# Attention and two feed-forward layers on one core: reloads behind their stores, two early tiles moved, the last tile transposed on TensorE

## The chip, the core and the metric

The kernel runs on one core of one Trainium2 chip. The metric is the device time of one execution in microseconds; smaller is better. A core has TensorE (PE; its weight loads are PEld), VectorE (DVE), ScalarE (ACT), GpSimd (POOL), SyncE (SP, which here only issues DMAs), SBUF as working memory, and PSUM, into which TensorE writes.

## What is computed

The input is attention data `q`, `k`, `v` of 4 x 8 x 576 x 64. The output of the attention is reshaped to 2304 rows (tokens) of 512 numbers, which go through two layers:

```python
x = ...                         # attention: a coarse part (4 positions averaged) + a local part (a band of 7)
h = x @ w_in                    # 512 -> 2048
g = h * tanh(softplus(h))
x = g @ w_out                   # 2048 -> 512
h = x @ moe2_w_in               # 512 -> 1024
solu = h * softmax(h)           # over the 1024 columns of a row
ln = (solu - mean) / sqrt(var + 1e-06) * g_ln
out = ln @ moe2_w_out           # 1024 -> 512
```

Attention and the first layer are not touched by the change; the second layer is.

## The kernel before

**Numbers.** Every matrix product is done with both operands split into a high and a low part of 32-bit "fp32r" numbers, and three products are added (`PASS`: high x high, high x low, low x high). So one tile of the second layer's input product is 2 x 12 matmuls of 512 columns, and one of its output product 24.

**First layer.** The 2304 tokens go in five blocks of 512, 384, 384, 512 and 512. A block has 16 chunks of the hidden dimension. A chunk is 12 matmuls into PSUM `h` (`chunk_in`, L631), an element-wise chain of five ACT and three DVE steps (L639 to L648), which ends with the cast L647 and the difference L648 that make the high and low half of `g`, and 12 matmuls into PSUM `y` (`chunk_out`, L659). At the end of a block `y` is copied out of PSUM with its sign turned, one half by ACT (L676), one by DVE (L673), and stored to the DRAM scratch `yscr` (`block_end`).

**Second layer.** Its weights are decoded beside the first layer, stored to scratch, loaded again and split (`second_split`, which calls `split`: cast L553 on ACT, difference L554 on DVE). Then 18 tiles of 128 tokens follow, each in two parts:

- `tile_in` (L682): load the tile from `yscr` into `qu` or `ku` by turns; split it (cast L691, difference L692 into `raw`); 24 matmuls (L700) into PSUM `y` (tiles 0 and 1: into two PSUM tiles `at`); row maximum L724 on DVE (L714 in tiles 0 and 1), exponential L726 (L719) on ACT, two products L729 on DVE, square with sum L737 on ACT, some small steps (L732 to L752), and the normalised tile, half by DVE (L759), half by ACT (L761). It has tokens on the partitions, and the output product needs the hidden dimension there. So it is stored to the scratch `zscr` (one DMA of 512 KB), loaded again in four DMAs of 128 KB that exchange 32 x 32 blocks, and transposed within the blocks by DVE (L771, two halves), each half followed by the cast L774 on ACT and the difference L775 on DVE, which make the two parts of `ln`.
- `tile_out` (L779): 24 matmuls (L787) of `ln` with the second weights, a copy L792 out of PSUM by ACT, and the store of the result.

All DMAs of this part are issued by SP through one helper (L266 in the profile).

**What sets the order.** No engine's order is written out by hand. Each step is recorded by `Plan.op` with an engine, a cost in us, a wanted time and the buffers that it reads and writes. `Plan.run` then plays the program through with these costs: whenever an engine is free, it takes, among the steps whose inputs are ready and for which buffers are free, the one wanted earliest. The order that results is the order in which the instructions are issued, engine by engine; on the chip each engine takes them strictly in this order. For a DMA `run` takes as its end the data time plus 1.3 us early in the program and 4.0 us later (`end = dma + (1.3 if now < 150 else 4.0)`). Wanted times are counted in chunks ("slots") of the first layer, 80 in all: tile `t` is wanted at `80 + 3 * (t - 2)`, but tiles 0 and 1 at 80 + `INTO[t]`, so among the last chunks, and the output part `G2LAG` = 10 later than the input part:

```python
INTO = (-5.5, -2.5)
s = 16 * NB + (INTO[t] if t < 2 else 3 * (t - 2))
pe(24 * 0.216, s + G2LAG, g2, [ln] + [w4t[k][0] for k in range(8)], [o])
```

## Time and profile before

| | |
|---|---|
| device time, median of 3 runs | 753.57 us (750.67 to 753.71) |
| the profiled execution | 748.23 us, of which 746.4 us are the profile's span |
| TensorE busy | 700.1 us (94%), mean granted clock 0.972 |
| DVE, ACT, POOL busy | 477.4, 484.2, 71.9 us |
| DMA | 99.40 MB, mean 133 GB/s |

The page gives the busy time of each engine; the chain in order of time shows, step by step backwards from the end, what released what; the waits list who waited for whom; the timeline shows instructions with the idle time before them and its releaser in brackets; the windows give the busy time and the granted TensorE clock (1.00 is full speed) of chosen stretches. A group "x24" is 24 instructions in a row. The second layer's tiles begin near 500 us, between the last chunks of the first layer.

### The profile page before, as it was taken

To read this page: it belongs to the slowest core of one execution; us is meant where nothing else is said; L and a number is where in the kernel's file an instruction comes from. 1 tells how busy PE (TensorE), PEld (TensorE's weight loads), DVE (VectorE), ACT (ScalarE), POOL (GpSimd) and SP (SyncE) were. 2 spreads that over 40 slices of the span, in tenths; PEclk is the share of its full clock that TensorE was granted. 3 is DMA by queue.
4 is the path that set the end of the run, shared out by engine and by line. 5 is a ranking of instruction groups with operands and counts; after the bars stand their busy time and mean duration, and the time that the engine had idled before them with its cause. 6 is when DMAs were issued, how large, how long until landed. Compare 5 with 4: busy or idle time off the path is not lost.

```text
span 746.4 us, 14379 instructions
## 1 busy us (share of the span) xinstructions
PE 700.1 (94%) x5576; PEld 585.4 (78%) x5576; DVE 477.4 (64%) x1040; ACT 484.2 (65%) x1143; POOL 71.9 (10%) x86
## 2 busy tenths in 40 slices
PE   3668999899999999999999999999999899999997
PEld 2456777799898899898788888888778688888875
DVE  6787897778745357665666665436645666666662
ACT  2785887677776687777686677667634554555542
POOL 2033333122310011200000000000000000000000
PEclk9757999999999999999999999999999999999999
DMA  8998764745623057643233314112234354345332
GB/s 243 264 289 210 184 140 106 261 99 134 123 49 111 18 125 190 161 142 130 79 105 122 103 43 161 67 69 68 88 114 142 111 156 143 130 138 169 128 113 99
DMA packets 76252, 99.40 MB, mean 133 GB/s; under 512 B 6616, under 2 KB 58712, under 8 KB 76184
## 3 DMA queue, kind: packets, MB, share of 16 engines
q1 hardware_dynamic: 64152, 84.66, 36.2%
q0 software_dynamic: 9440, 9.10, 8.5%
q10 hardware_dynamic: 2592, 4.72, 1.6%
q8 instruction: 44, 0.72, 0.4%
q14 instruction: 24, 0.20, 0.1%
HBM read 74.34 MB, written 24.12 MB: 132 GB/s over the span
## 4 chain that ended last, share of the span: by engine, by line
PE 80%; DMA 6%; ACT 5%; DVE 5%; issue 2%; SPq 1%; POOL 0%; ACTq 0%; POOLq 0%
PE h L631 24%; PE y L659 23%; PE at L787 13%; PE y L700 12%; DMA qkd<-in_qkc_dram 2%; PE at L410 2%; DMA wi<-in_w_dram 2%; DMA wo<-in_vc_dram 2%; PE at L700 1%; SPq L266 1%; PE at L484 1%; ACT sm L374 1%; PE at L353 1%; PE at L526 1%; PE at L513 1%
## 5 line engine op out<-in xcount | busy, mean ns | idle before, releaser
L631 PE MATMUL h<-x,wi 128*128 128x512 f32 (+1 forms) x960 | 215.7, 374 | 5.8 <-DVE e L645 5.7
L659 PE MATMUL y<-g,wo 128*128 128x512 f32 (+1 forms) x960 | 218.4, 374 | 1.8 <-ACT g L647 1.2
L631 PEld LDWEIGHTS h<-x,wi 128*128 128x128 f32 x960 | 174.5, 189 | 32.5 <-DVE e L645 8.1
L659 PEld LDWEIGHTS y<-g,wo 128*128 128x128 f32 x960 | 173.3, 189 | 27.6 <-ACT g L647 2.0
L787 PE MATMUL at<-wi,wo 128*128 128x512 f32 x432 | 103.4, 395 | 6.1 <-ACT wo L774 6.0
L787 PEld LDWEIGHTS at<-wi,wo 128*128 128x128 f32 x432 | 81.7, 190 | 25.7 <-ACT wo L774 7.2
L700 PE MATMUL y<-wi,raw 128*128 128x512 f32 x384 | 89.4, 389 | 0.8 <-ACT vu L676 0.8
L700 PEld LDWEIGHTS y<-wi,raw 128*128 128x128 f32 x384 | 72.0, 188 | 16.1 <-ACT vu L676 1.2
L639 ACT ACTIVATE e<-h 128x512 f32<-128x512 f32 (+1 forms) x80 | 44.1, 551 | 54.5 <-PE h L631 54.0
L645 DVE SCALAR_TENSOR_TENSOR e<-e,h 128x512 f32<-128x512 f32 (+1 forms) x80 | 50.4, 631 | 33.6 <-ACT e L644 33.0
L641 ACT ACTIVATE e<-e,ones 128x512 f32<-128x512 f32 (+1 forms) x80 | 54.3, 680 | 17.8 <-DVE e L640 17.5
L648 DVE TENSOR_TENSOR g<-e,g 128x512 fp32r<-128x512 f32 (+1 forms) x80 | 50.7, 635 | 22.6 <-ACT g L647 22.0
L647 ACT CAST g<-e 128x512 fp32r<-128x512 f32 (+1 forms) x80 | 45.9, 575 | 27.9 <-DVE e L645 27.7
L640 DVE TENSOR_SCALAR e<-e 128x512 f32<-128x512 f32 (+1 forms) x80 | 31.8, 397 | 43.3 <-ACT e L639 43.1
L643 ACT ACTIVATE e<-e,ones 128x512 f32<-128x512 f32 (+1 forms) x80 | 54.2, 679 | 1.6
L264 POOL DMA_DIRECT2D qkd<-in_qkc_dram x36 | 35.5, 996 | 133.7 <-DMA qkd<-in_qkc_dram 79.7
L644 ACT ACTIVATE e<-e 128x512 f32<-128x512 f32 (+1 forms) x80 | 46.9, 586 | 1.1
L726 ACT ACTIVATE wo<-y,nm 128x1024 f32<-128x1024 f32 x16 | 17.9, 1116 | 37.4 <-DVE nm L724 37.4
L264 POOL DMA_DIRECT2D vd<-in_vc_dram x36 | 36.3, 1020 | 58.5 <-DMA vd<-in_vc_dram 37.7
L374 ACT ACTIVATE sm<-sm,nm 128x40 f32<-128x40 f32 x120 | 37.6, 315 | 4.8 <-DVE nm L368 4.8
L737 ACT ACTIVATE wo<-wo,mv 128x1024 f32<-128x1024 f32 x18 | 20.7, 1152 | 22.7 <-DVE mv L732 22.7
L729 DVE SCALAR_TENSOR_TENSOR wo<-wo,y 128x512 f32<-128x512 f32 x32 | 21.7, 683 | 17.8 <-ACT wo L726 17.8
(151 smaller groups left out, 806.3 us busy)
## 6 DMA issues: line engine op xcount, KB each, us to landing
raw<-in_w_dram SPq DMA_DIRECT2D x24, 512.0 KB
zscr<-wo SPq DMA_DIRECT2D x18, 512.0 KB
wo<-zscr SPq DMA_DIRECT2D x72, 128.0 KB
wi<-in_w_dram SPq DMA_DIRECT2D x6, 1024.0 KB
wo<-in_w_dram SPq DMA_DIRECT2D x6, 1024.0 KB
qkd<-in_qkc_dram POOLq DMA_DIRECT2D x36, 144.0 KB, 4.7
ku<-in_ku_dram SPq DMA_DIRECT2D x15, 320.0 KB
vu<-in_vu_dram SPq DMA_DIRECT2D x60, 80.0 KB
```

Source lines behind the costliest of these rows:

```text
L264: return op("pool", nbytes / DMA_RATE, want, lambda: nc.gpsimd.dma_start(out_(), in_(), accum_op=ALU.add), r, w, after=after)
L374: nc.scalar.activation(heads()[:, i, :], heads()[:, i, :], AF.Exp, bias=nm()[:, i:i + 1], accum_out=su()[:, i:i + 1])
L631: mm(h()[:, :N], w()[:, f % 2, a, 128 * c:128 * c + 128], x()[:, b, c, :N], start=(n == 0), stop=(n == 11))
L641: act(act_us(N, 0.09), s + 0.1, lambda: nc.scalar.activation(e(), e(), AF.Square, bias=ones()[:, 0:1]), [ones], [eb])
L643: lambda: nc.scalar.activation(e(), e(), AF.Ln, scale=0.5, bias=ones()[:, 1:2]), [ones], [eb])
L644: act(act_us(N), s + 0.1, lambda: nc.scalar.activation(e(), e(), AF.Exp, scale=-1.0), [], [eb])
L645: dve(dve_us(N), s + 0.2, lambda: nc.vector.scalar_tensor_tensor(e(), e(), 1.0, h()[:, :N], op0=ALU.subtract, op1=ALU.mult), [h], [eb])
L647: act(act_us(N), s + 0.2, lambda: nc.scalar.copy(g()[:, 0, :N], e()), [eb], [g])
L648: dve(dve_us(N), s + 0.2, lambda: nc.vector.tensor_tensor(g()[:, 1, :N], e(), g()[:, 0, :N].bitcast(F32), op=ALU.subtract), [eb], [g])
L659: mm(y[d2]()[:, d, :N], w()[:, f % 2, a, c:c + 128], g()[:, b, :N], start=(f == fs[0] and n == 0), stop=(f == fs[-1] and n == 2))
L700: mm(part(m), x()[:, a, c, :], w()[:, i, b, :], start=(n == 0), stop=(n == 11))
L787: mm(o(), ln()[:, a, k, :], w()[:, i, b, :], start=(n == 0), stop=(n == 23))
```

## The change

Four things are changed in the plan's inputs, and one in what is computed where.

- `op` and `dma` take a `lag` for SP's DMAs, the time that the plan adds behind the data. The store to `zscr` gets 0.3 and the four reloads 1.0 in place of 4.0, so that in the plan a reload becomes ready soon after its store.
- `INTO` becomes (-7, -0.9): tile 0 is wanted earlier, tile 1 later.
- The output part of tiles 0 and 1 is wanted 8 instead of 10 slots behind their input part.
- The last tile (t = 17) is not stored and loaded again. It is normalised into its plain order, transposed by eight TensorE transposes of 128 x 128 into two PSUM tiles `h`, and cast (L780 of the changed kernel) and differenced (L781) from there.

```diff
--- before.py
+++ after.py
@@ -42,7 +42,7 @@
 NEXT = {0: (0.0, 6.0, -3.0, 0.8), 26: (-3.0, 4.0, -14.0, 2.0), 32: (2.0, 10.0, 4.0, 1.2), 48: (2.0, 10.0, 4.0, 1.2)}
 WANT = [0, 2, 4, 6, 8, 13, 16, 20]
 G2LAG = 10
-INTO = (-5.5, -2.5)
+INTO = (-7, -0.9)
 DMA_RATE = 270e3
 LAG = 0.15
 AHEAD = 2
@@ -99,7 +99,6 @@
         self.ops = []
 
     def op(self, eng, cost, want, fn, r=(), w=(), lag=None, after=(), join=False):
-        lag = LAG if lag is None else lag
         n = len(self.ops)
         deps = set(after)
         for b in r:
@@ -169,10 +168,10 @@
                     if eng in ("sp", "pool"):
                         at[eng] = now + (0.45 if eng == "sp" else 1.1)
                         dma = max(dma, at[eng] + 1.2) + cost
-                        end = dma + (1.3 if now < 150 else 4.0)
+                        end = dma + ((1.3 if now < 150 else 4.0) if lag is None else lag)
                     else:
                         at[eng] = now + cost
-                        end = at[eng] + lag
+                        end = at[eng] + (LAG if lag is None else lag)
                         heapq.heappush(done, (at[eng], pick, True))
                     heapq.heappush(done, (end, pick, False))
             nxt = [t for e, t in at.items() if t > now and ready[e]]
@@ -257,13 +256,13 @@
     yparts = [[Buf(None, None, None, 0) for _ in range(2)] for _ in range(NB)]
     wparts = [Buf(None, None, None, 0) for _ in range(8)]
 
-    def dma(want, out_, in_, r=(), w=(), nbytes=0, accum=False, after=(), pool=False, join=False):
+    def dma(want, out_, in_, r=(), w=(), nbytes=0, accum=False, after=(), pool=False, join=False, lag=None):
         if pool:
             return op("pool", nbytes / DMA_RATE, want, lambda: nc.gpsimd.dma_start(out_(), in_()), r, w, after=after, join=join)
         elif accum:
             return op("pool", nbytes / DMA_RATE, want, lambda: nc.gpsimd.dma_start(out_(), in_(), accum_op=ALU.add), r, w, after=after)
         else:
-            return op("sp", nbytes / DMA_RATE, want, lambda: nc.sync.dma_start(out_(), in_()), r, w, after=after, join=join)
+            return op("sp", nbytes / DMA_RATE, want, lambda: nc.sync.dma_start(out_(), in_()), r, w, lag, after, join)
 
     def dve(cost, want, fn, r, w, after=()):
         return op("dve", cost, want, fn, r, w, after=after)
@@ -754,17 +753,39 @@
         act(0.35, s + 0.3, root, [], [r])
         dve(0.6, s + 0.4, stat, [mv], [r])
         ln = S([128, 2, 8, 128], "wo", 8, F32R)
-        turned = lambda m: ez()[:, 1].rearrange("t (g k f) -> t g k f", g=4, k=8)[:, :, 4 * m:4 * m + 4]
-        flat = lambda m: e()[:, m].rearrange("t (k g f) -> t g k f", k=4, g=4)
+        last = t == NTI - 1
+        flat = lambda m: e()[:, m] if last else e()[:, m].rearrange("t (k g f) -> t g k f", k=4, g=4)
+
+        def turned(m):
+            if last:
+                return ez()[:, 1, 512 * m:512 * m + 512]
+            return ez()[:, 1].rearrange("t (g k f) -> t g k f", g=4, k=8)[:, :, 4 * m:4 * m + 4]
+
         dve(dve_us(512), s + 0.4, lambda: nc.vector.tensor_scalar(
             turned(0), flat(0), mv()[:, 2:3], y(), op0=ALU.add, op1=ALU.mult), [mv, r], [ez])
         act(act_us(512), s + 0.4, lambda: nc.scalar.activation(
             turned(1), flat(1), AF.Identity, bias=c(), scale=y()), [r], [ez])
-        dma(s + 0.5, lambda: zscr[t], lambda: ez()[:, 1], r=[ez], w=[zs], nbytes=524288)
+        if last:
+            for m in range(2):
+                tp = P("h")
+                ks = slice(4 * m, 4 * m + 4)
+
+                def flip(m=m, tp=tp):
+                    for k in range(4):
+                        nc.tensor.transpose(tp()[:, 128 * k:128 * k + 128],
+                                            turned(m)[:, 128 * k:128 * k + 128], ident())
+
+                pe(0.43, s + 0.9, flip, [ez, ident], [tp])
+                v = lambda tp=tp: tp().rearrange("f (k t) -> f k t", k=4)
+                act(act_us(512), s + 0.9, lambda v=v, ks=ks: nc.scalar.copy(ln()[:, 0, ks, :], v()), [tp], [ln])
+                dve(dve_us(512), s + 0.9, lambda v=v, ks=ks: nc.vector.tensor_tensor(
+                    ln()[:, 1, ks, :], v(), ln()[:, 0, ks, :].bitcast(F32), op=ALU.subtract), [tp], [ln])
+            return ln
+        dma(s + 0.5, lambda: zscr[t], lambda: ez()[:, 1], r=[ez], w=[zs], nbytes=524288, lag=0.3)
         for g in range(4):
             dma(s + 0.6, lambda g=g: zv()[32 * g:32 * g + 32],
                 lambda g=g: zscr[t].rearrange("(a t) (g f) -> g t a f", a=4, g=4)[g],
-                r=[zs, ez], w=[zv], nbytes=131072, join=True)
+                r=[zs, ez], w=[zv], nbytes=131072, join=True, lag=1.0)
         for m in range(2):
             ks = slice(4 * m, 4 * m + 4)
             v = lambda ks=ks: ez()[:, 1].rearrange("p (k t) -> p k t", k=8)[:, ks]
@@ -787,7 +808,7 @@
                     mm(o(), ln()[:, a, k, :], w()[:, i, b, :], start=(n == 0), stop=(n == 23))
                     n += 1
 
-        pe(24 * 0.216, s + G2LAG, g2, [ln] + [w4t[k][0] for k in range(8)], [o])
+        pe(24 * 0.216, s + (8 if t < 2 else G2LAG), g2, [ln] + [w4t[k][0] for k in range(8)], [o])
         os_ = S([128, 512], "ys", 2)
         act(act_us(512), s + 1.6, lambda: nc.scalar.copy(os_(), o()), [o], [os_])
         op("act", 0.1, s + 1.6, lambda: nc.scalar.dma_start(out[128 * t:128 * t + 128, :], os_()), [os_], (), lag=5.0)
```

The instructions themselves are otherwise the same; what else changes is their order, which the plan makes. The order up to TensorE's row 254 is the same in both. Lines of the changed kernel up to L755 are one less than before (L699 is L700 before), the two halves of the normalised tile are L764 and L766 (L759 and L761 before), the transposes, casts and differences L792, L795 and L796 (L771, L774, L775), the output product L808 (L787).

TensorE at the end of the last block, before (`h` and `y` are the first layer's chunks, `y<-wi,raw` and `at<-wi,raw` a second-layer tile's input product, `at<-wi,wo` its output product; x24 is one tile):

```order
L659 MATMUL y<-g,wo 128x512 x12
L631 MATMUL h<-x_4658,wi 128x512 x12
L659 MATMUL y<-g,wo 128x512 x24
L700 MATMUL y<-wi,raw 128x512 x48
L787 MATMUL at<-wi,wo 128x512 x48
```

and with the change:

```order
L658 MATMUL y<-g,wo 128x512 x12
L630 MATMUL h<-x_4658,wi 128x512 x12
L699 MATMUL at<-wi,raw 128x512 x24
L658 MATMUL y<-g,wo 128x512 x24
L699 MATMUL y<-wi,raw 128x512 x24
L808 MATMUL at<-wi,wo 128x512 x24
L699 MATMUL y<-wi,raw 128x512 x48
```

Tile 1's input product now stands between the last `h` and the last 24 `y` matmuls, and behind these one input and one output product follow in place of two and two.

SP in the first tiles, before (`zscr<-wo` is a tile's store, `wo<-zscr` with the same number its four reloads, `ku`, `qu<-yscr` the load of a later tile; wo_6139 and wo_6194 are tiles 2 and 3):

```order
L266 DMA ku_6188<-yscr_66 128x4x128
L266 DMA zscr_68<-wo_6139 128x1024
L266 DMA zscr_68<-wo_6194 128x1024
L266 DMA wo_6139<-zscr_68 32x4x256 x4
L266 DMA qu_6310<-yscr_66 128x4x128
L266 DMA wo_6194<-zscr_68 32x4x256 x4
```

and with the change (wo_6044, wo_6147 and wo_6225 are tiles 1, 2 and 3):

```order
L265 DMA wo_6044<-zscr_68 32x4x256 x4
L265 DMA zscr_68<-wo_6147 128x1024
L265 DMA ku_6220<-yscr_66 128x4x128
L265 DMA wo_6147<-zscr_68 32x4x256 x4
L265 DMA qu_6277<-yscr_66 128x4x128
L265 DMA zscr_68<-wo_6225 128x1024
```

Each tile's reloads now follow its own store, ahead of the next tile's store. DVE in the same place, before (L724 is the row maximum of tile 5, L771 the transposes of tile 2, L729 the products of tile 5):

```order
L724 TENSOR_REDUCE nm2_6338<-y_6294 128x1
L740 SCALAR_TENSOR_TENSOR r2_6342<-mv_6327,su2_6313 128x1
L771 STREAM_TRANSPOSE wo_6139<-wo_6139 128x4x4x32
L729 SCALAR_TENSOR_TENSOR wo_6344,mv_6350<-wo_6344,y_6294 128x512
L775 TENSOR_TENSOR wo_6348<-wo_6139,wo_6348 128x512
L749 TENSOR_SCALAR r2_6342<-r2_6342 128x1
L750 TENSOR_SCALAR r2_6342<-r2_6342 128x1
L751 TENSOR_TENSOR r2_6342<-r2_6342 128x1
L752 TENSOR_TENSOR r2_6342<-r2_6342,mv_6327 128x1
```

and with the change, from right behind the row maximum of tile 4 (L792 are the transposes of tile 2, L728 the products of tile 4, L748 to L764 the normalisation of tile 3, L691 the low half of tile 5's input):

```order
L792 STREAM_TRANSPOSE wo_6147<-wo_6147 128x4x4x32
L728 SCALAR_TENSOR_TENSOR wo_6284,mv_6292<-wo_6284,y_6207 128x512
L748 TENSOR_SCALAR r2_6282<-r2_6282 128x1
L749 TENSOR_SCALAR r2_6282<-r2_6282 128x1
L750 TENSOR_TENSOR r2_6282<-r2_6282 128x1
L751 TENSOR_TENSOR r2_6282<-r2_6282,mv_6241 128x1
L796 TENSOR_TENSOR wo_6294<-wo_6147,wo_6294 128x512
L764 TENSOR_SCALAR wo_6225<-wo_6225,mv_6241,r2_6282 128x4x128
L792 STREAM_TRANSPOSE wo_6147<-wo_6147 128x4x4x32
L728 SCALAR_TENSOR_TENSOR wo_6284,mv_6292<-wo_6284,y_6207 128x512
L733 TENSOR_SCALAR su2_6285<-su2_6285 128x1
L691 TENSOR_TENSOR raw_6290<-ku_6220,raw_6290 128x512
```

The transposes of tile 2 have come from behind tile 5's row maximum to behind tile 4's, and they stand ahead of the low half of tile 5's input.

TensorE at the end of the program, before (the last 96 are the outputs of tiles 14 to 17):

```order
L700 MATMUL y<-wi,raw 128x512 x24
L787 MATMUL at<-wi,wo 128x512 x24
L700 MATMUL y<-wi,raw 128x512 x12
L787 MATMUL at<-wi,wo 128x512 x96
L923 UNCONDITIONAL_BRANCH
```

and with the change:

```order
L808 MATMUL at<-wi,wo 128x512 x24
L699 MATMUL y<-wi,raw 128x512 x24
L808 MATMUL at<-wi,wo 128x512 x48
L775 MATMUL h<-ident,wo 128x128 x8
L808 MATMUL at<-wi,wo 128x512 x48
```

The eight transposes of tile 17 stand between the outputs of tiles 15 and 16.

## Rows read from the trace of the kernel before

**Rows 1.** The page's head and its part 1: busy us, share, instructions.

```profile
span 746.4 us, 14379 instructions
...
PE 700.1 (94%) x5576; PEld 585.4 (78%) x5576; DVE 477.4 (64%) x1040; ACT 484.2 (65%) x1143; POOL 71.9 (10%) x86
```

**Rows 2.** Waits of TensorE, 490 to 747 us: total us, times, longest.

```profile
PE at L787 <- ACT wo L774: 6.0, 3, 3.1
PE y L659 <- ACT g L647: 1.2, 1, 1.2
```

**Rows 3.** Chain in order of time, 495 to 560 us: start, us, what.

```profile
495.66 2.72 PE y L659 x12
...
536.46 2.73 PE h L631 x12
...
543.85 0.70 DVE g L648
...
546.06 0.60 ACT vu L676
546.66 0.94 ACT wi L553
...
548.15 11.17 PE y L700 x48
```

**Rows 4.** Chain in order of time, around tile 2's output.

```profile
570.20 10.89 PE y L700 x48
...
591.87 5.44 PE y L700 x24
```

**Rows 5.** Windows: stretch, its us, busy by engine, clock, DMA share, GB/s.

```profile
570.00:581.00 11.00, 11.00 (x49) 8.82 (x48) 3.09 (x9) 3.62 (x6) 0.00 (x0) 1.00 0.85 214
...
587.00:589.00 2.00, 2.00 (x6) 1.61 (x5) 2.00 (x7) 1.59 (x3) 0.00 (x0) 0.50 0.24 96
```

**Rows 6.** Timeline of DVE, 581 to 590 us: start, us, instruction, idle before.

```profile
581.12 1.23 DVE L724 TENSOR_REDUCE nm<-y 128x1 f32<-128x1024 f32 x1 [1.33 <-PE y L700]
...
582.32 0.70 DVE L771 STREAM_TRANSPOSE wo<-wo 128x512 f32<-128x512 f32 x1
583.62 0.69 DVE L729 SCALAR_TENSOR_TENSOR wo<-wo,y 128x512 f32<-128x512 f32 x1 [0.59 <-ACT wo L726]
...
587.25 0.69 DVE L775 TENSOR_TENSOR wo<-wo 128x512 fp32r<-128x512 f32 x1
...
588.63 0.68 DVE L692 TENSOR_TENSOR raw<-qu,raw 128x512 fp32r<-128x512 f32 x1
```

**Rows 7.** Chain in order of time, the tail.

```profile
714.27 2.73 PE y L700 x12
...
742.89 0.59 ACT ys L792
```

**Rows 8.** Timeline of ACT and DVE in the tail.

```profile
721.23 1.15 ACT L737 ACTIVATE wo<-wo,mv 128x1024 f32<-128x1024 f32 x1 [1.74 <-DVE mv L732]
...
726.23 0.81 ACT L761 ACTIVATE wo<-wo,r 128x512 f32<-128x512 f32 x1
...
735.14 0.71 DVE L771 STREAM_TRANSPOSE wo<-wo 128x512 f32<-128x512 f32 x1 [3.10 <-DMA wo<-zscr]
```

**Rows 9.** Timeline of SP: tile 17's store and reloads, and a tile's load earlier.

```profile
695.29 0.52 SPq L266 DMA_DIRECT2D ku<-yscr  x1
...
727.07 0.34 SPq L266 DMA_DIRECT2D zscr<-wo  x1
...
729.71 2.76 SPq L266 DMA_DIRECT2D wo<-zscr  x4
```

**Rows 10.** Windows: the steady part of the second layer.

```profile
600.00:715.00 115.00, 115.00 (x509) 95.21 (x508) 78.33 (x206) 59.44 (x116) 0.00 (x0) 1.00 0.44 139
```

**Rows 11.** Timeline of TensorE: transposes of the attention, then the next matmuls.

```profile
106.99 0.66 PE L392 MATMUL at<-ident,wi 128*128 128x128 f32 x4
107.40 0.94 PE L631 MATMUL h<-x,wi 128*128 128x512 f32 x3
```

## Prediction

> **What bounds the kernel now.** I read the page's parts 1 and 2 first: TensorE is busy 700.1 of 746.4 us [rows 1]. A change that removes no matmul can therefore only win back TensorE's idle time, and only where it idles after the point at which the two orders part. They part late: the first 254 rows of TensorE's order are the same in both kernels, and the first row that differs runs at 495.66 us [rows 3]. So I read the waits of TensorE from 490 us to the end: 6.0 us, in three waits, for the scalar engine's cast L774 of the transposed tile, the longest 3.1, and 1.2 for the last chunks' cast L647 [rows 2]. Then the chain in order of time shows what each of these places costs beyond the wait itself. The measure is that 24 matmuls at full clock take 5.44 us [rows 4], so one takes 0.227.
>
> (a) The end of the last block. The last `h` matmuls end at 536.46 + 2.73 = 539.19 [rows 3]. Behind them only the 24 `y` matmuls are left, which wait for the element-wise chain of the last chunk; that chain's last step ends at 543.85 + 0.70 = 544.55. Then tile 2 needs the PSUM of `y`, and its two copies L676 have the weight split L553 (0.94 us) between them. Tile 2 starts at 548.15. That is 8.96 us for 5.44 us of matmuls: **3.5 us lost**.
>
> (b) The output matmuls of tile 2. They could begin when the inputs of tiles 4 and 5 are done, at 570.20 + 10.89 = 581.09, and the next row after them starts at 591.87 [rows 4]: 10.78 us for 24 matmuls, **5.3 us lost**. 3.06 of it is the wait [rows 2]. The rest is the clock: in the stretch after the wait the granted clock is 0.50, the lower of the two levels (1.2 GHz of 2.4), and before the wait TensorE had run without a gap at 1.00 [rows 5]. DVE shows why the tile is late: its first transpose L771 runs at 582.32, right behind the row maximum L724 of a later tile, which had to wait for TensorE until 581.12 [rows 6].
>
> (c) The tail. The input of tile 17 ends at 714.27 + 2.73 = 717.00 and the last output matmul at 742.89 [rows 7]. Four tiles of output matmuls are 21.76 us, the stretch is 25.9: **4.1 us lost**, among it the wait for tile 17, whose transpose stood 3.1 us waiting for the reload [rows 8]. The store was issued at 727.07, the last reload was issued by 732.47, and the transpose began at 735.14, 8.07 us after the store [rows 9].
>
> Together 3.5 + 5.3 + 4.1 = 12.9 us, the most that any reordering behind 496 us can bring. Between 600 and 715 us TensorE is busy all of the time [rows 10].
>
> **The change, part by part.**
>
> Tile 0 one chunk earlier. It needs the first four weight splits. These stand in the common prefix, and TensorE did not wait for them [rows 2]; the order after them on ACT and DVE first differs at tile 0's own work. I price the earlier place at 0. Its cover is the chunk order: as before, one tile's statistics run beside one chunk. If that cover failed, it would be a wait like the one of 1.2 us in [rows 2].
>
> Tile 1 between the last `h` and the last `y` matmuls. This puts 5.44 us of matmuls in front of the wait in (a). The chain of the last chunk ended 544.55 - 539.19 = 5.4 us after the last `h`, and its matmuls would now come at 5.44 + 2.72 = 8.2, so 2.8 us of cover remain. Against it stands what tile 1's own statistics put ahead of it, two half maxima on DVE and two half exponentials on ACT, each pair about the 1.2 us of a whole L724 or L737 [rows 6, 8]. The weight split now stands ahead of both copies L676. The first `y` half was complete at 546.04 and the second at about 547.4; two copies back to back end at about 547.2, so tile 2 follows without a gap. Gain 3.5.
>
> The order of the first tiles. Now one tile goes out between tile 2 and tile 3, and tile 2's output comes behind the inputs of tiles 3, 4, 5 and the outputs of tiles 0 and 1: 27.2 us after its own input, nearly the same distance as before (581.09 less 553.6). What changes is what stands ahead of its transposes. On SP the reload of tile 2 now follows its store with one tile load between; before, the store of tile 3, which waits for tile 3's statistics, stood between. On DVE the transposes are ready to run when the maximum of tile 4 is done, one output and one input group (10.88 us) before they are needed. So the 5.3 us of (b) go, the clock's part with them.
>
> What is late next is the input of tile 5. Its low half, L691 of the changed kernel (L692 before), stands on DVE behind the maximum of tile 4, both transposes of tile 2 and both products of tile 4. The same instructions stood in one piece before: from the maximum at 581.12 to the first product at 583.62 are 2.50 us, from there through product, difference L775, the four small ones from L749, transpose, L759 and second product to 587.25 are 3.63, and L692 is 0.68 [rows 6]; with 0.07 for one small instruction more, 6.9 us after the input of tile 4 ends. TensorE spends 5.44 us on tile 1's output meanwhile, and tile 5's first two matmuls (0.45) need only the high half. It therefore waits about 6.95 - 5.9 = **1.1 us**. No row of before shows this wait. Bounds: 0, if the exponential returns sooner, and 5.3 with the clock falling, as in (b). I take 1.1, since it is nearest to the 1.2 of [rows 2], behind which no lower clock stood in the chain, while behind the 3.06 one did.
>
> Steady state. SP's store, wait, reload and next tile load take 2.64 + 2.76 + 0.52 = 5.9 us [rows 9] of a tile's 10.88, and DVE is busy 78.33 of 115 us [rows 10]. A tile's transposes now stand one tile (10.88 us) behind that tile's normalisation, so some 10.4 us behind its store; 8.07 are needed [rows 9]. Price 0, with 2.3 us of cover.
>
> The tail. The last tile's store, four reloads and two DVE transposes go; eight TensorE transposes are added, behind the output of tile 15. Four transposes took 0.41 us from start to the next matmul (106.99 to 107.40) [rows 11], so eight take **0.8**; the longest reading of the same row, 0.66 each four, gives 1.3. The tile is normalised 726.23 + 0.81 = 727.04 before, 10.0 us after the input's end. In the new order the square L737 stands behind the copy of tile 14's output (which ends at about 6.1 of this scale), and 726.23 + 0.81 - 721.23 = 5.8 us lie between its start and the normalised tile [rows 8], so 11.9 at most; two foreign ACT steps of about 0.5 and a DVE queue of about 1 in that stretch are gone, so about 10. TensorE is through with tile 15 at 10.9, and the transposes wait 0 to 1 us; I take 0. Tile 15's first half is now transposed ahead of tile 17's maximum, tile 16's halves right behind tile 17's normalised half. Tile 16's second half is ready some 3.6 us behind that, at 13.6 (two transposes, two casts and two differences with one of tile 17 between them, taking turns on DVE and ACT at 0.6 to 0.7 us); TensorE asks for it at 10.9 + 0.8 + 2.7 = 14.4. Gain 4.1 - 0.8 = 3.3.
>
> Sum: -3.5 - 5.3 + 1.1 - 3.3 = -11.0 us. The profiled execution took 748.23 us (span 746.4 and 1.8 around it), so it would be 737.2. The runs shown have a median of 753.57, 5.3 above it; nothing in one profile tells where those lie, so I carry them on: **742.6 us**.
>
> A rule speaks against the change. The Trainium skill, "DMA: Bandwidth & Descriptors", section "Rules for kernel authors", says to issue a transfer early, compute, and wait for it late. By it, a reload right behind its store would expose the store's time, 2.64 us in each of some 14 tiles, 37 us in all, and the result would be 780 us. The rows stand against that: SP is free for almost half of each tile, and what it holds back is loaded a tile ahead.
>
> **Rivals.**
>
> B, the wait at tile 5 grows and brings the lower clock with it. For it: DVE has no gap there, and any delay of tile 2's reload adds one to one. Against it: 1.1 is far from 3.06. It then costs 5.3 instead of 1.1, the gain is 6.8, and the time 746.8.
>
> C, the other side: the shorter cover of the reload. DVE runs in order, and a tile's transposes now stand ahead of the next tile's maximum. If store and reload took longer than 10.4 us, everything behind would wait in every tile. It decides from about 10.4 + 3.5 = 13.9 us, when DVE's idle share (32% of 10.88) is used up too; 2 us more would cost 14 x 2 = 28 us and give 771. Against it: 8.07 in the only row where a transpose waited for its reload. The rule above would come out on this side.
>
> D, the tail is not relieved: the square behind the copy makes the transposes late, or tile 16's second half is. Then 3.3 us of the gain stay away: 745.9. For it: margins of about 1 us. Against it: a margin missed by 1 costs 1, not 3.
>
> E, B and D together, or a chunk held up by tile 0: a gain of 3.5 or less, 750 or more. That the change doesn't do what it says is excluded by the order, which shows the eight transposes and the moved tiles.
>
> **How the numbers follow.** Forecast 0.66, B 0.13, D 0.10, E 0.07, C 0.04. About 0.5% (3.8 us) is what a measurement of this kernel can tell from no change. Forecast, B and D lie below 749.8; a little is taken off for B and D at a high run: faster 0.88, same 0.08 (E and that rest), slower 0.04 (C). The low end is the lowest run less all 12.9: 737.8. The high end is B on the highest run, 753.71 - 6.8 = 746.9, and half the spread of the runs, 1.5: 748.4. Left out are E and C and some edges, under 0.2.
>
> **What would show it.** TensorE's waits behind 496 us: none for L647 or the copies of `y`, none for the cast of the transposed tiles, one of 0.5 to 2 us in tile 5's input for L691. The granted clock 1.00 from 500 us to the end. From the end of tile 17's input to the last output matmul about 22.6 us instead of 25.9. A wait of TensorE above 3 us, transposes that wait for reloads in many tiles, or a `y` matmul waiting for `g` between 496 and 545 us would prove it wrong.

## The result and the profile after

The changed kernel took **743.79 us**, the median of four executions (741.93 to 748.06), beside 753.1 us for the kernel before in the same comparison (750.67 to 753.71). The ratio is 0.989 with a 95% interval of 0.9842 to 0.9939: faster by 1.1%. The forecast was 742.6 us, in a range of 737.8 to 748.4.

The page's head and part 1 of the changed kernel's profile, for [rows 1]:

```profile
span 745.9 us, 14393 instructions
...
PE 700.8 (94%) x5584; PEld 589.1 (79%) x5584; DVE 475.3 (64%) x1038; ACT 485.7 (65%) x1143; POOL 71.6 (10%) x86
```

This execution took 748.06 us, almost exactly the 748.23 us of the profiled execution before. Read by the span alone, the change would have brought nothing. So the trace has to be read from the point at which the orders part. The chain in order of time (start, us, what), 500 to 595 us:

```profile
505.71 5.44 PE at L699 x24
...
541.07 2.72 PE h L630 x12
543.79 5.44 PE at L699 x24
549.23 5.44 PE y L658 x24
554.67 5.56 PE y L699 x24
560.23 5.44 PE at L808 x24
565.67 10.89 PE y L699 x48
...
583.54 5.30 PE y L699 x22
588.84 5.44 PE at L808 x24
```

The first row that differs starts at 505.71 us, where it started at 495.66 before [rows 3]: TensorE's 4545 matmuls ahead of it, in the same order in both, took 10.05 us longer in this execution. That this differs from execution to execution of one kernel, the last experiment shows. Behind it the two kernels can be compared. I call **the stretch** the time from the first row that differs to the end of the last output matmul:

- before: 495.66 to 742.87 (the copy behind it starts at 742.89 [rows 7]), 247.2 us;
- after: 505.71 to 731.15 + 10.92 = 742.07 (chain of the tail, below), 236.4 us.

That is 10.8 us less, where the sum of the prediction had 11.0. The stretch is 234 us of matmuls at full clock (1032 of 0.2267 us) in both kernels; what stands above that was 13.3 us and is now 2.4. The single places:

The waits of TensorE, 490 to 747 us (total us, times, longest), for [rows 2]:

```profile
PE y L699 <- DVE raw L691: 1.1, 1, 1.1
```

This is the only one left; the waits for the casts and for the last chunk are gone. In the chain above, tile 1's input (543.79), the last `y` matmuls (549.23) and tile 2's input (554.67) follow one another without a gap: loss (a) is gone. The new wait stands between 576.56, where the x48 group ends, and 583.54, with the 24 output matmuls and two input matmuls of tile 5 between. DVE's timeline shows it step by step (start, us, instruction, idle before), for [rows 6]:

```profile
576.59 1.23 DVE L723 TENSOR_REDUCE nm<-y 128x1 f32<-128x1024 f32 x1 [0.72 <-PE y L699]
...
577.80 0.71 DVE L792 STREAM_TRANSPOSE wo<-wo 128x512 f32<-128x512 f32 x1
579.09 0.69 DVE L728 SCALAR_TENSOR_TENSOR wo<-wo,y 128x512 f32<-128x512 f32 x1 [0.58 <-ACT wo L725]
...
582.15 0.65 DVE L728 SCALAR_TENSOR_TENSOR wo<-wo,y 128x512 f32<-128x512 f32 x1
...
582.80 0.68 DVE L691 TENSOR_TENSOR raw<-ku,raw 128x512 fp32r<-128x512 f32 x1
```

The low half of tile 5 is done at 582.80 + 0.68 = 583.48, 6.92 us behind the end of tile 4's input; the prediction had 6.9. The first of TensorE's matmuls that need it starts at 583.54, 1.1 us late, and the 22 of that group take 5.30 us where 22 x 0.2267 are 4.99: the place costs 1.4 us in all.

The tail, in the chain, for [rows 7]:

```profile
713.96 5.44 PE y L699 x24
719.40 10.88 PE at L808 x48
730.28 0.87 PE h L775 x8
731.15 10.92 PE at L808 x48
...
742.10 0.59 ACT ys L813
```

From the end of tile 17's input, 719.40, to the last output matmul, 742.07, are 22.67 us in place of 25.9, of which the eight transposes are 0.87. Two rows, of ACT's and of DVE's timeline, show how near it was, for [rows 8]:

```profile
728.19 0.82 ACT L766 ACTIVATE wo<-wo,r 128x512 f32<-128x512 f32 x1 [0.92 <-DVE r L751]
```

```profile
732.03 0.68 DVE L796 TENSOR_TENSOR wo<-wo 128x512 fp32r<-128x512 f32 x1
```

The normalised tile 17 is there at 729.01, 1.27 us before the transposes start. The second half of tile 16 is there at 732.71, and TensorE asks for it 0.87 + 2.72 us behind 730.28, at 733.87.

The windows around the new wait (stretch, its us, busy by engine, clock, DMA share, GB/s), for [rows 5]:

```profile
576.00:582.00 6.00, 6.00 (x28) 4.99 (x27) 4.72 (x12) 3.67 (x8) 0.00 (x0) 1.00 0.00 0
583.50:586.00 2.50, 2.46 (x11) 2.03 (x12) 1.49 (x5) 2.10 (x4) 0.00 (x0) 1.00 0.80 313
```

The granted clock stays at 1.00 behind a wait of 1.1 us.

### The profile page after: what moved, and what is told of

Read it like the earlier page. It is cut to its first block, busy times and chain, and to the rows that moved or that the text cites. A ratio compares the mean times of both kernels' runs of the same rounds, so it can differ in the third digit from the quotient of the medians.

```text
span 745.9 us, 14393 instructions
## 1 busy us (share of the span) xinstructions
PE 700.8 (94%) x5584; PEld 589.1 (79%) x5584; DVE 475.3 (64%) x1038; ACT 485.7 (65%) x1143; POOL 71.6 (10%) x86
## 4 chain that ended last, share of the span: by engine, by line
PE 85%; DVE 4%; ACT 4%; DMA 4%; issue 2%; SPq 1%; ACTq 0%
PE h L630 26%; PE y L658 25%; PE at L808 12%; PE y L699 12%; PE at L409 3%; DMA ku<-in_ku_dram 2%; PE at L699 1%; DMA g<-in_qu_dram 1%; PE at L352 1%; PE at L483 1%; SPq L265 1%; PE at L525 1%; PE at L512 1%; DMA vu<-in_vu_dram 1%; PE at L391 1%
## 5 line engine op out<-in xcount | busy, mean ns | idle before, releaser
L630 PEld LDWEIGHTS h<-x,wi 128*128 128x128 f32 x960 | 176.3, 191 | 33.3 <-DVE e L644 8.6
L808 PE MATMUL at<-wi,wo 128*128 128x512 f32 x432 | 100.6, 389 | 0.0
L808 PEld LDWEIGHTS at<-wi,wo 128*128 128x128 f32 x432 | 81.0, 188 | 16.8
L699 PE MATMUL y<-wi,raw 128*128 128x512 f32 x384 | 89.9, 390 | 1.1 <-DVE raw L691 1.1
L699 PEld LDWEIGHTS y<-wi,raw 128*128 128x128 f32 x384 | 71.9, 188 | 16.7 <-DVE raw L691 1.5
L813 ACT COPY ys<-at 128x512 f32<-128x512 f32 x18 | 10.6, 589 | 41.3 <-PE at L808 41.3
L540 DVE TENSOR_SCALAR ys<-ys 128x512 f32<-128x512 f32 (+1 forms) x36 | 18.6, 517 | 17.4 <-ACT ys L539 17.3
```

The source lines that it names most:

```text
L630: mm(h()[:, :N], w()[:, f % 2, a, 128 * c:128 * c + 128], x()[:, b, c, :N], start=(n == 0), stop=(n == 11))
L699: mm(part(m), x()[:, a, c, :], w()[:, i, b, :], start=(n == 0), stop=(n == 11))
L808: mm(o(), ln()[:, a, k, :], w()[:, i, b, :], start=(n == 0), stop=(n == 23))
```

## The experiments: the change taken apart

The change has three parts: **lags** (0.3 and 1.0 for the store and the reloads), **places** (`INTO` and the 8 slots), **transposes** (tile 17 by TensorE). Every combination was run. These three edits of the changed kernel undo one part each, and the kernels below are named by the parts that they keep:

```diff
-        dma(s + 0.5, lambda: zscr[t], lambda: ez()[:, 1], r=[ez], w=[zs], nbytes=524288, lag=0.3)
+        dma(s + 0.5, lambda: zscr[t], lambda: ez()[:, 1], r=[ez], w=[zs], nbytes=524288, lag=None)
...
-                r=[zs, ez], w=[zv], nbytes=131072, join=True, lag=1.0)
+                r=[zs, ez], w=[zv], nbytes=131072, join=True, lag=None)
```

```diff
-INTO = (-7, -0.9)
+INTO = (-5.5, -2.5)
...
-        pe(24 * 0.216, s + (8 if t < 2 else G2LAG), g2, [ln] + [w4t[k][0] for k in range(8)], [o])
+        pe(24 * 0.216, s + G2LAG, g2, [ln] + [w4t[k][0] for k in range(8)], [o])
```

```diff
-        last = t == NTI - 1
+        last = False
```

All of them share the rows up to the one where the stretch begins. What they gave, with the losses read from each chain as the prediction reads them before: (a) from the last `h` to tile 2's input less 5.44; "middle" what goes beyond full matmul groups around the first output products and tile 5; "tail" from tile 17's input to the last matmul less 21.76.

| parts kept | stretch | (a) | middle | tail | ratio to before (95%) |
|---|---|---|---|---|---|
| none (before) | 247.2 | 3.5 | 5.3 | 4.1 | 1 |
| lags | 240.0 | 2.8 | 0 | 3.2 | 0.9896 (0.9846 to 0.9946) |
| places | 240.0 | 0 | 1.9 | 4.1 | 0.9907 (0.986 to 0.9953) |
| transposes | 250.9 | 3.5 | 5.3 | 7.8 | 1.0022 (0.9971 to 1.0073) |
| lags, places | 240.5 | 0 | 1.4 | 5.0 | 0.9882 (0.9802 to 0.9962) |
| lags, transposes | 237.8 | 2.8 | 0 | 0.9 | 0.9897 (0.983 to 0.9964) |
| places, transposes | 242.6 | 0 | 1.9 | 6.8 | 0.9888 (0.9831 to 0.9945) |
| all | 236.4 | 0 | 1.4 | 0.9 | 0.989 (0.9842 to 0.9939) |

The ratios cannot tell the six faster ones apart, since their intervals are 0.9 to 1.6% wide; the stretch can. It is read from one profiled execution of each; the two kernels that were profiled twice repeat it to 0.1 us (last experiment).

**Lags alone.** Expected:

> Only the shorter lags of the store and the reloads (tiles 0 and 1 at their old places, tile 17 stored and reloaded). Read from the end of the last row that both orders share (495.66 us before, 505.71 after) to the end of the last matmul: 247.2 us before, 236.4 after. Theory 1 (each loss goes with one part of the change; the lags carry loss (b), tile 2's output): (b), 5.3 us, goes, no wait for L795 around tile 2's output; (a) 3.5 us and the tail 4.1 us stay: 247.2 - 5.3 = 241.9. Theory 2 ((b) goes because one output now stands between the inputs of tiles 2 and 3, which the moved tiles bring): (b) stays, 247.2. Theory 3 (the lags order everything, the rest is decoration): about 237.

Measured: 746.09 us median, stretch 499.36 to 739.36. Loss (b) is gone, so the lags carry it, as theory 1 has it. The stretch is 1.9 us shorter than its 241.9: (a) came out 0.7 smaller, as the weight split on ACT now stood behind both copies of `y` and not between them, and the tail 0.9 smaller. Theories 2 and 3 fall.

**Places alone.** Expected:

> Only the places of tiles 0 and 1 and the 8 slots (old lag of 4.0, tile 17 stored and reloaded). Theory 1 (the lags carry (b)): (a) goes, (b) stays with a wait of about 3 us and the lower clock, tail stays: 247.2 - 3.5 = 243.7. Theory 2 (the places relieve (b) too): 247.2 - 3.5 - 5.3 = 238.4, with at most 1 or 2 us of small waits at tile 2's output on top. In both no wait for L647 and none for the copies of y at the end of the last block.

Measured: 744.0 us, stretch 498.87 to 738.86. (b) is nearly gone here too, with the old lags. TensorE's timeline around the output product behind the inputs of tiles 3 and 4:

```profile
558.63 11.04 PE L699 MATMUL y<-wi,raw 128*128 128x512 f32 x48
570.28 0.73 PE L808 MATMUL at<-wi,wo 128*128 128x512 f32 x2 [0.60 <-ACT wo L795]
571.66 5.34 PE L808 MATMUL at<-wi,wo 128*128 128x512 f32 x22 [0.65 <-DVE wo L796]
```

Two short waits, 1.9 us beyond the full group, and no slower matmuls behind them. So theory 1 is wrong in that the lags alone carry (b): either part removes most of it, and the 5.3 us can be won only once.

**Transposes alone.** Expected:

> Only tile 17's transposes by TensorE (old lags and places). Theory 1 (the transposes themselves relieve the tail, as they replace store, reload and DVE transposes): the 4.1 us become 0.8, 247.2 - 3.3 = 243.9. Theory 2 (they need the order that the lags make): here they stand behind one output product after tile 17's input, 5.44 us, and tile 17 is normalised only 10 us after its input, so TensorE waits about 4.5 us in front of them; with 0.8 for themselves that is 5.3 in place of 4.1, 248.4, and more if the clock falls behind that wait. (a) and (b) stay in both.

Measured: 753.96 us, no gain. The profiled execution was a long one (761.68 us, first differing row at 505.21); the stretch behind that is 250.9 us, 3.7 more than before. TensorE's timeline of the tail (the x18 are the part of a group of 24 that falls into the window asked for):

```profile
727.73 4.24 PE L808 MATMUL at<-wi,wo 128*128 128x512 f32 x18
735.80 1.96 PE L775 MATMUL h<-ident,wo 128*128 128x128 f32 x8 [3.83 <-DVE wo L764]
737.41 18.64 PE L808 MATMUL at<-wi,wo 128*128 128x512 f32 x72
```

Theory 2 holds, and it costs more than it said: a wait of 3.83 us, then transposes and matmuls at the lower clock, 1.96 us for eight (0.87 in the changed kernel) and from their end 18.3 us for 72 matmuls that take 16.3 at full clock. Here the eight stand one output product behind tile 17's input, not two.

**Lags and places, without the transposes.** Expected:

> Lags and places as in the change, but tile 17 stored, reloaded and transposed by DVE. Theory 1 (the tail's gain is the transposes'): 236.4 + 3.3 = 239.7, with one wait for tile 17's cast of about 3 us near the end. Rival (the tail was late because of tiles 15 and 16, which the lags move; the transposes add nothing): 236.4 - 0.8 = 235.6, no wait above 1 us in the tail.

Measured: 745.12 us, stretch 499.39 to 739.85, 240.5. The tail waits for the reload of tile 17 (timeline of TensorE, then the windows):

```profile
732.25 7.59 PE L808 MATMUL at<-wi,wo 128*128 128x512 f32 x24 [2.60 <-ACT wo L795]
```

```profile
734.00:736.00 2.00, 2.00 (x6) 1.63 (x5) 0.69 (x1) 0.19 (x1) 0.00 (x0) 0.50 0.00 0
```

The clock is at 0.50, the lower of its two levels, behind the 2.60 us, and 24 matmuls take 7.59. Theory 1 holds; the transposes are worth 5.0 - 0.9 = 4.1 us here. The rival, that tiles 15 and 16 alone made the tail late, falls.

**Lags and transposes, without the places.** Expected:

> Lags and transposes as in the change, tiles 0 and 1 at their old places. Theory 1 (the places are worth (a) alone): (a) stays, the wait at tile 5's input goes because its neighbours are others: 236.4 + 3.5 - 1.1 = 238.8; if that wait stays, 239.9. Rival (the places carry (b) too): 236.4 + 3.5 + 5.3 = 245.2 or a little less.

Measured: 744.68 us, stretch 500.83 to 738.58. Theory 1 within 1.1 us: (a) is back with 2.8, the wait at tile 5 is gone, the tail is as in the changed kernel. So the places are worth only 1.4 us beside the other two: they win 2.8 at the block's end and pay 1.4 at tile 5.

**Places and transposes, without the lags.** Expected:

> Places and transposes as in the change, old lag of 4.0. Theory 1 (the parts of the stretch add: what the places alone left, 240.0, and in the tail what the transposes alone made, 7.8 us lost for 4.1): 240.0 + 3.7 = 243.7, with a wait of about 3.8 us in front of the transposes. Rival (with the places moved, tiles 15 to 17 stand otherwise and the transposes need no lags): 240.0 - 3.3 = 236.7, no wait in front of the transposes.

Measured: 742.87 us, stretch 495.24 to 737.88, 242.6. The longest wait of TensorE from 490 us on:

```profile
PE h L775 <- DVE wo L764: 3.8, 1, 3.8
```

Theory 1 holds within 1.1 us: the transposes wait 3.8 us again. What makes them a gain is the order that the lags bring, in which the outputs of tiles 14 and 15, and not of 14 alone, stand in front of them.

## The experiments: how far the cover of the reload reaches

The prediction gave the reload 2.3 us of cover and let rival C decide at 13.9 us from store to transpose. Here each tile's store is issued two or three times in a row, with the same data, which moves the reload by one or two stores; the plan and TensorE's order stay as they are:

```diff
-        dma(s + 0.5, lambda: zscr[t], lambda: ez()[:, 1], r=[ez], w=[zs], nbytes=524288, lag=0.3)
+        op("sp", 524288 / DMA_RATE, s + 0.5, lambda: [nc.sync.dma_start(zscr[t], ez()[:, 1]) for _ in range(2)], [ez], [zs], 0.3)
```

Two stores, expected:

> The changed kernel, each tile's store to the scratch issued twice in a row, the same data, so that the reload starts one store later: 0.34 + 2.38 = 2.72 us in the changed kernel's SP rows. The plan's order is the same. Theory 1 (2.3 us of cover behind the reload and some 3.5 us of idle DVE in each tile): the transposes are ready 8.07 + 2.72 = 10.8 us after the first store, 0.4 behind their place, which DVE's idle time takes up: below 6 us over all the tiles, the stretch 236.4 to 242, small waits. Rival C (the cover is already used up, each us of a later reload goes onto the path): 15 x 2.7 = 41 us more.

Three stores (`range(3)`), expected:

> The same with three stores: the reload 5.44 us later, the transposes ready 13.5 us after the first store, 3.1 us behind their place. Theory 1 (rival C decides from 10.4 + 3.5 = 13.9 us): the small waits grow, but the loss stays well below one for one, 5 to 15 us. Rival (DVE's idle time is itself made of waits for ScalarE and TensorE and gives no cover): 15 x 3.1 = 46 us more than the changed kernel.

Measured: two stores 745.9 us (ratio to before 0.992, 0.988 to 0.996), stretch 500.20 to 739.56, 239.4; three stores 789.34 us in one execution, stretch 503.34 to 783.82, 280.5. The second store cost 3.0 us in all, as theory 1 has it; the third 41 more, and there theory 1 (5 to 15 us) is wrong. The rival's 46 is near in number only, since it spreads the loss evenly over 15 tiles. Read in three pieces, from the chains and TensorE's timelines, it lies as follows (us; the stretch up to the start of tile 6's input, from there to the end of tile 17's input, and the tail behind that):

| stores | to tile 6's input | tiles 6 to 17 | tail | stretch |
|---|---|---|---|---|
| one | 88.6 | 125.1 | 22.7 | 236.4 |
| two | 90.0 | 125.1 | 24.3 | 239.4 |
| three | 98.0 | 142.6 | 39.9 | 280.5 |

With two stores the steady tiles lose nothing. With three they lose 17.5 us, the first tiles 9.4 (with waits of TensorE of 2.4, 2.1 and 3.7) and the tail 17.2. What SP waited for tells why the steady tiles lose (L784 are the stores that are issued several times, L265 all other DMAs). The changed kernel, SP's waits from 600 to 700 us:

```profile
SPq L265 <- DVE wo L764: 47.2, 9, 5.5
SPq L265 <- DMA zscr<-wo: 23.5, 10, 2.7
```

With two stores, 600 to 700 us:

```profile
SPq L784 <- DMA zscr<-wo: 26.8, 10, 3.7
SPq L265 <- DMA zscr<-wo: 23.7, 10, 3.3
SPq L784 <- DVE wo L764: 20.8, 10, 5.6
```

With three, 600 to 760 us:

```profile
SPq L784 <- DMA zscr<-wo: 72.8, 25, 4.0
SPq L265 <- DMA zscr<-wo: 31.9, 12, 4.1
SPq L784 <- DVE wo L764: 9.6, 2, 5.7
```

A wait of SP for the normalised tile (`wo L764`) is time in which SP has nothing to do. It is 47.2 / 9 = 5.2 us for a tile in the changed kernel, 2.1 with two stores, and with three it has vanished from all but two tiles. SP's timeline in the changed kernel, one round:

```profile
642.43 0.34 SPq L265 DMA_DIRECT2D zscr<-wo  x1
645.15 1.73 SPq L265 DMA_DIRECT2D wo<-zscr  x4
646.92 0.52 SPq L265 DMA_DIRECT2D ku<-yscr  x1
```

and with three stores:

```profile
627.97 7.38 SPq L784 DMA_DIRECT2D zscr<-wo  x3
638.48 1.74 SPq L265 DMA_DIRECT2D wo<-zscr  x4
640.26 0.52 SPq L265 DMA_DIRECT2D qu<-yscr  x1
640.88 7.09 SPq L784 DMA_DIRECT2D zscr<-wo  x3
```

A round's work, from the store at 642.43 to the end of the tile load at 647.44, is 5.0 us in the changed kernel. With three stores one round, 627.97 to 640.88, is 12.9 us, longer than a tile's 10.88, and the eight from 627.97 to 728.90 are 12.6 each. TensorE's timeline with three stores, the inputs of tiles 8, 16 and 17 and the last three outputs:

```profile
625.30 5.60 PE L699 MATMUL y<-wi,raw 128*128 128x512 f32 x24
725.85 5.63 PE L699 MATMUL y<-wi,raw 128*128 128x512 f32 x24
738.32 5.63 PE L699 MATMUL y<-wi,raw 128*128 128x512 f32 x24
755.43 8.46 PE L808 MATMUL at<-wi,wo 128*128 128x512 f32 x24 [4.45 <-ACT wo L795]
770.69 13.11 PE L808 MATMUL at<-wi,wo 128*128 128x512 f32 x48 [5.46 <-ACT wo L795]
```

From tile 8 to tile 16 a tile takes (725.85 - 625.30) / 8 = 12.6 us too. So in the steady tiles SP, which there waits almost only for its own transfers, sets the pace, 1.7 us a tile above the 10.88. In the tail no input products are left between the outputs: TensorE waits 4.45 and 5.46 us for casts of the last tiles, which in the chain stand behind their stores and reloads, and behind both waits the granted clock is 0.50. Whether SP's round or DVE's place would limit first at a smaller delay was not tried.

The rule quoted in the prediction (the Trainium skill, "DMA: Bandwidth & Descriptors", section "Rules for kernel authors": issue early, compute, wait late) was priced there at 37 us for a reload right behind its store. The trace of the changed kernel does not agree with that price: the 23.5 us that SP waits for its own stores cost TensorE nothing. With three stores, where SP has no idle time left, such waits do reach TensorE.

**The lag too short.** Lags of -1.0, so that the plan has the reload before it can be there:

```diff
-        dma(s + 0.5, lambda: zscr[t], lambda: ez()[:, 1], r=[ez], w=[zs], nbytes=524288, lag=0.3)
+        dma(s + 0.5, lambda: zscr[t], lambda: ez()[:, 1], r=[ez], w=[zs], nbytes=524288, lag=-1.0)
...
-                r=[zs, ez], w=[zv], nbytes=131072, join=True, lag=1.0)
+                r=[zs, ez], w=[zv], nbytes=131072, join=True, lag=-1.0)
```

> The changed kernel with lags of -1.0 for the store and the reloads, so the plan puts the transposes still earlier and pairs the tiles: on DVE both tiles' transposes stand right behind the second one's normalised half and ahead of the next product steps. A transpose is ready some 7.9 us after its store. Theory 1 (a lag that is too short brings rival C's waits: DVE stands in front of the second tile's transpose for several us, once in two tiles, and TensorE waits behind it): 1 to 5 us for each of some 7 pairs, the stretch 243 to 271. Theory 2 (the sooner the plan has the reload, the better; DVE's idle time takes the rest): 236.4 or less.

Measured: 758.17 us in one execution, stretch 505.20 to 752.55, 247.4. DVE's waits, 560 to 745 us, of this kernel and then of the changed one:

```profile
DVE wo L792 <- DMA wo<-zscr: 32.4, 12, 5.6
```

```profile
DVE wo L792 <- DMA wo<-zscr: 0.8, 1, 0.8
```

Theory 1 holds: DVE stands in front of transposes whose reload has not landed, and all 11 us that the change wins are lost. This is rival C's mechanism, reached by the order alone.

## The experiments: the last wait, and the first 500 us

Tile 5's two halves are wanted 5 slots earlier:

```diff
-        act(act_us(512), s - 1, lambda: nc.scalar.copy(x()[:, 0], xf()), [xf], [x])
-        dve(dve_us(512), s - 1, lambda: nc.vector.tensor_tensor(
+        act(act_us(512), s - (6 if t == 5 else 1), lambda: nc.scalar.copy(x()[:, 0], xf()), [xf], [x])
+        dve(dve_us(512), s - (6 if t == 5 else 1), lambda: nc.vector.tensor_tensor(
```

> The changed kernel with the two halves of tile 5's input wanted 5 slots earlier, so that L691 stands ahead of one difference, the second transpose and the second product of that piece of DVE's order. Theory 1 (tile 5's 1.1 us wait is DVE's queue): the wait goes, the stretch 236.4 - 1.1 = 235.3; in the time of an execution 0.15%, less than can be measured. Rival (a later tile's split, now in another order, takes over the wait): 236.4 or more.

Measured: stretch 500.57 to 735.50, 234.9. TensorE now has no wait behind 490 us, and the chain there is matmuls alone. Theory 1 holds: the 1.1 us wait is gone, and with it the 0.3 us by which the group behind it was longer, so 1.4 in place of 1.1. The median, 740.17 us, was 3.6 lower than the changed kernel's, far more than 1.4 us of stretch explain, so both went side by side once more. The changed kernel, unedited:

> The changed kernel once more, beside early5_again on the same chip. The profiled executions so far reached the point at which the orders part between 495.7 us (before) and 505.7 us (the changed kernel), with the same rows up to there. Theory 1 (that difference is from execution to execution): here it is reached between 496 and 506 and most likely near 500, while the stretch behind it repeats 236.4 within 0.3 us. Rival (the changed kernel itself makes its first 500 us longer, through another order on ScalarE, VectorE or SP): again 505 to 506.

And the one with the earlier split:

> Tile 5's input split earlier, again, beside the changed kernel. Theory 1 (it saves the 1.1 us wait and its neighbours, 1.4 us in the stretch, and its lower median of 740.2 us was made by the first 500 us): stretch 234.9, and a time within 0.5% of the changed kernel's in this call. Rival (the 3.6 us between the medians are its own): again 0.5% faster than the changed kernel or more.

Measured: the changed kernel 736.06 us (six executions, 733.66 to 744.25; ratio 0.9818, 0.9751 to 0.9885), the other 741.91 us (735.53 to 746.34; ratio 0.9869, 0.9812 to 0.9926). The stretches repeat to 0.1 us: 493.56 to 729.88, 236.3, and 494.58 to 729.51, 234.9. The rival of early5_again falls, since the medians have changed sides; theory 1's 0.5% was missed too: the earlier split was 0.8% slower here. Over all executions the changed kernel has a median of 741.1 us (ten) and the earlier split 741.4 (twelve): the 1.4 us are there in the trace and cannot be seen in the time.

The same kernel thus reached its first differing row at 505.71 in one execution and at 493.56 in another; over the 14 profiled executions of this study, all with 4545 matmuls of TensorE up to there, it was 493.6 to 505.7. The windows of the first 260 us, the earlier profiled execution of the changed kernel and then the later:

```profile
0.00:260.00 260.00, 220.91 (x2361) 185.99 (x2362) 183.18 (x362) 179.71 (x484) 58.57 (x72) 0.89 0.62 160
```

```profile
0.00:260.00 260.00, 229.43 (x2420) 193.51 (x2421) 187.19 (x369) 187.03 (x496) 59.26 (x72) 0.93 0.62 160
```

Here the difference arises: less of TensorE's time is busy, and at a lower clock. By the end of this window all of it is there: the same 24 `y` matmuls start at 255.43 in the earlier execution and at 243.17 in the later, 12.3 us apart. So the rival of changed_again, that the change itself makes this part longer, falls, though its theory 1 (496 to 506) was missed by 2.4 us to the low side. Why one execution waits more there than another was not tried.

## Why the prediction was right

Step by step, by its own terms:

- **(a) -3.5.** Right: no gap, and without the places it is back (2.8 to 3.5 in the four kernels without them).
- **(b) -5.3.** Right in the sum: no wait for the cast and no lower clock around tile 2's output. The reason given, the reload behind its own store and the transposes earlier on DVE, is right for the lags, but is not the only one: the places alone leave 1.9 of the 5.3.
- **Tile 5, +1.1.** The wait measured 1.1, from a queue of 6.92 us against 6.9; the place costs 1.4, with the 22 matmuls behind the wait. Rival B, that this wait grows and brings the lower clock, did not come: the clock stayed at 1.00.
- **Tail, -3.3.** Right, 3.2: 25.9 became 22.67, with 0.87 for the transposes (0.8 taken) and no wait in front of them. The margins were there as worked out: tile 17 normalised 9.6 us behind its input (about 10), the second half of tile 16 at 13.3 (13.6), asked for at 14.5 (14.4). Rival D did not come. What the prediction did not say is that this term hangs on the lags: without them the transposes wait 3.8 us and the tail is worse than before.
- **The steady state at 0.** Right: in the changed kernel DVE waits for a reload once, 0.8 us.
- **From the profiled execution to the median, +5.3.** This was carried on without a reason. The first 500 us are the likely one: the profiled execution before reached the first differing row at 495.66, early in the range of 493.6 to 505.7, and the one after at its very end. It is not shown, since the other executions behind the two medians have no trace. That the median came within 1.2 us of the forecast is therefore partly luck: the same kernel, measured again as changed_again, had 736.06 us, below the low end of 737.8. What the traces show is the 10.8 us in the stretch.

No step that the forecast rests on failed. What the record does not bear out is the outlook around rival C: "It decides from about 10.4 + 3.5 = 13.9 us, when DVE's idle share ... is used up too", from which the expectation for three stores took 5 to 15 us. There the transposes were to be ready at 13.5 us, and 44.1 us were lost. The run is no clean test of the 13.9, since the stores themselves became slower and a transpose ran at 642.90, 14.9 us behind its first store of 627.97, outside the bound. But the bound speaks of DVE alone, and the trace shows two limits beside it: SP's round, 5.0 us of a tile's 10.88 in the changed kernel and 12.6 with three stores, which takes 1.7 us from each of the tiles 8 to 16, and the tail, where the late reloads and the lower clock behind them took 17.2 us. It did not touch the forecast, since with one store SP idles 5.2 us in each tile.

## What to carry to other kernels

Read a change from the point where the two orders part, not from the span: here the same kernel moved by 12 us ahead of that point, more than the whole change was worth behind it. Losses that share a cause cannot be added up over the parts of a change, and a part that is a gain in one order can be a loss in another, so a step put on TensorE needs enough matmuls between its input and itself. For a queue that issues, waits and issues again, its cover is the time in which it waits for its producer (here 5.2 us a tile); when that is gone, its round sets the pace, here 12.6 us a tile with three stores.

## What was not expected

The granted clock behind a wait near the end of the second layer: after 1.1 us (the changed kernel), two waits of 0.60 and 0.65 us in short order (places alone) and 2.35 us (lags alone) the rows show 1.00; after 2.60 (without the transposes), 3.06 (before [rows 5]) and 3.83 us (transposes alone, and places with transposes) they show 0.50. The length of the last wait alone does not sort them: with three stores a wait of 1.75 us, followed two matmuls later by one of 0.32, has 0.50 behind it (696.5 to 698.5 us), and one of 1.85, followed by 0.32 in the same way, has 1.00 (670.9 to 673.0). A fall costs about 1.6 us on top of the wait: the last 24 matmuls took 7.59 us behind the 2.60, and 6.01 behind the 2.35, where the clock stayed at 1.00. Only these rows are known; what lies between them was not tried.
